# Linear attention and two MLPs on one core: weight conversion in halves, the order of the first loads, the due times of the combining sums, and the last product's steps

## The chip, the cores and the metric

One core of one Trainium2 chip. The metric is device time in microseconds (us) of one execution, the median of several.

## What is computed

```python
# q, k, v: (8, 8, 576, 64) float32
q_s = exp(q - max(q, -1));  q_s /= sum(q_s, -1) + 1e-9          # over the head's 64 columns
k_s = exp(k - max(k, 2));   k_s /= sum(k_s, 2) + 1e-9           # over the 576 positions
x   = q_s @ (k_s^T @ v)                                         # linear attention, -> 4608 x 512
h   = x @ w_in;  g = h * clip(h + 3, 0, 6) / 6;  y = g @ w_out  # 512 x 2048, 2048 x 512
xn  = y / sqrt(mean(y*y, -1) + 1e-6) * rms_g
out = (silu(xn @ w_gate) * (xn @ w_val)) @ w_out2               # 512 x 1536 (two), 1536 x 512
```

The five weight matrices arrive as 64-bit floating-point numbers (two 32-bit words each); q, k and v are float32.

## The kernel before

Every float32 product is made of three matmuls on values split in a high and a low part ("hi" and "lo", `xh`/`xl`, `phu`/`plu`, `gh`/`gl`, `uh`/`ul`): high by high, low by high, high by low. ScalarE (ACT) makes the high part by a cast (line 215), VectorE (DVE) or GpSimd (POOL) the low part by a subtraction (line 221).

The 4608 tokens are nine blocks of 512. One batch of the attention (`kv_tasks`, line 1069) loads five tiles of k (`k_0` to `k_4`), folds them to a maximum on DVE (`km`, lines 355 to 358), transposes that on TensorE (PE; `kmt`, line 368), subtracts the maximum (lines 389, 391), takes the exponential on ACT (line 395) and multiplies with v on PE (`kvp`, line 411, 80 matmuls). `q_tasks` (line 1101) does the same for q by rows (`qm` line 503, exponential line 509, `qn` line 519, transposition `qp` line 531), and `xps` (line 551) is the attention's result of a block.

A weight tile of 128 x 512 is converted to float32 on chip in `weight` (line 1036): load of the raw pairs (`raw_*`, line 235), two ACT operations (`conv_a`, lines 258 and 259), four DVE operations each on the result of the one before (`conv_d`, lines 266 to 269: clamp, shift and mask, a two-input operation that puts the words together, mask), a multiplication (`conv_p`, line 274, POOL) and an addition (`conv_s`, line 278, DVE or POOL). There are 68 such tiles: 16 of w_in, 28 of w_out and w_out2 (both appear as `wm_out`, `w_out`), 24 of w_gate and w_val (`wm_gv`, `w_gv`).

Blocks 0 to 2 go through the first MLP directly: steps `m1` (tile `h`, line 603) and `m2` (tile `y`, line 662). Blocks 3 to 8 take a two-by-two scheme that needs seven products instead of eight for w_in (`prod1`, tiles `phx`, `phy`, `phz`, line 833). The second MLP does the same with w_gate and w_val (`prod`, tiles `pux`, `puy`, `puz`, line 851) for pairs of blocks S = 0 to 3 and the last block alone as S = 4, in 12 groups of seven products each, 60 in all. The seven products of a group share three of the four rotating PSUM banks x, y, z; between two products that reuse a bank, ACT copies (`c_copy`, line 866, here called p1) and DVE adds (`c_add`, lines 868 to 873: `c12`, `c21`, `c22`) what the bank holds, and the next product waits for that. The last product is the step `m4` (tile `o`, line 962, 12 matmuls of 128x512 each); 12 of them belong to each block, and one can run once its u is there. `swu` (line 759) are sums of w_gate and w_val tiles that the scheme multiplies with.

Order of the work: the PE's order is written out as the list `seq` (lines 986 to 1017). `merge` (line 980) puts other steps between the seven products of a group. All other work is tasks of a list scheduler, `Plan` (line 40), which replays the program by costs in us and gives each engine, as it comes free, the ready task with the earliest due time, in units of PE steps, if there is room for its buffers. What it writes down is fixed in the program: each engine then works through its list in that order, and waits in place for what it needs. An entry "FLEX" may go to POOL or to DVE. Loads are all on SyncE's (SP) queue.

## Time and profile before

| | |
|---|---|
| three runs | 1773.12, 1773.75, 1774.95 us (median 1773.75) |
| profiled execution | 1766.21 us |
| its span (first to last instruction) | 1764.3 us |
| mean granted TensorE clock | 0.992 |
| busy, share of the span | PE 96%, DVE 73%, ACT 49%, POOL 20% |
| busiest queue | SP's 16 engines 61%, 199 GB/s over the span |

The profiled execution took 1766.21 us, 1.91 us more than its span and 7.54 us less than the median of the runs. In a row of the timeline the columns are start, time from there to the end of the last instruction of the row, engine, line, operation, output and inputs, number of instructions, and in square brackets the idle time of the engine before it and what ended that. Times in windows are from the span's start. A granted clock of 1.00 is the upper of TensorE's two levels (2.4 GHz), one of 0.50 the lower (1.2 GHz).

### The profile page before, as it was taken

How to read it: one execution, taken by the hardware profiler on the slowest of the kernel's cores; microseconds unless marked ns; L12 is line 12 of the kernel's file. 1: busy time of each engine (PE TensorE's matmuls, PEld its weight loads, DVE VectorE, ACT ScalarE, POOL GpSimd, SP SyncE). 2: the span in 40 equal slices, each digit the busy share in tenths (PEclk: the TensorE clock that was granted, in tenths of full speed). 3: DMA queues.
4: the chain of work that ended last, by engine and by line, in shares of the span. 5: the costliest groups of instructions: out<-in, count | busy, mean ns of one | idle time of the engine just before them, and what ended most of it. 6: DMA issues, size and time to landing. Idle time of an engine off the chain costs nothing. (4 is left out here: it accounts for less than half of the span.)

```text
span 1764.3 us, 26397 instructions
## 1 busy us (share of the span) xinstructions
PE 1697.6 (96%) x9166; PEld 1438.2 (82%) x9166; DVE 1294.8 (73%) x2202; ACT 866.3 (49%) x2018; POOL 348.7 (20%) x326
## 2 busy tenths in 40 slices
PE   4799999999999999999999999999999999999999
PEld 3577787788888898998987777888888888888997
DVE  8999777787878787878689999445754475546564
ACT  7864546555564747545355545333432344243342
POOL 2243320011211111222123343111211121111000
PEclk9799999999999999999999999999999999999999
DMA  9646376797878788576695454535453545354752
GB/s 257 188 140 209 138 255 234 269 287 244 243 224 272 207 264 261 191 245 232 199 327 163 169 197 153 189 104 191 142 188 105 182 158 182 111 173 155 264 186 83
DMA packets 189093, 351.98 MB, mean 200 GB/s; under 512 B 26016, under 2 KB 90016, under 8 KB 188960
## 3 DMA queue, kind: packets, MB, share of 16 engines
q1 hardware_dynamic: 188960, 350.30, 61.0%
q8 instruction: 73, 1.20, 0.3%
q14 instruction: 60, 0.49, 0.1%
HBM read 285.74 MB, written 64.49 MB: 199 GB/s over the span
## 5 line engine op out<-in xcount | busy, mean ns | idle before, releaser
L962 PE MATMUL o<-wv,uh 128*128 128x512 f32 x864 | 266.5, 390 | 0.0
L962 PEld LDWEIGHTS o<-wv,uh 128*128 128x128 f32 x864 | 161.0, 188 | 32.5
L221 POOL TENSOR_TENSOR plu<-pg,phu 128x512 fp32r<-128x512 f32 (+1 forms) x63 | 85.4, 1356 | 442.5 <-ACT phu L215 403.1
L962 PE MATMUL o<-wv,ul 128*128 128x512 f32 x432 | 168.0, 389 | 0.0
L662 PE MATMUL y<-gl,hout 128*128 128x512 f32 x360 | 141.9, 394 | 4.8 <-POOL gl L221 3.9
L662 PE MATMUL y<-gh,hout 128*128 128x512 f32 x360 | 144.8, 402 | 0.8 <-DVE ysb L677 0.4
L851 PE MATMUL puy<-xhu,phu 128*128 128x512 f32 (+1 forms) x360 | 133.8, 372 | 10.8 <-DVE c12u L873 8.3
L662 PE MATMUL y<-gh,wo 128*128 128x512 f32 x432 | 143.1, 392 | 1.0 <-DMA wo<-rdout 1.0
L215 ACT ACTIVATE phu<-pg 128x512 fp32r<-128x512 f32 x240 | 130.7, 569 | 23.4 <-DMA pg<-pd 23.4
L662 PE MATMUL y<-gh,lout 128*128 128x512 f32 x360 | 141.3, 393 | 0.0
L851 PE MATMUL puy<-xlu,phu 128*128 128x512 f32 (+1 forms) x360 | 132.5, 368 | 0.0
L851 PE MATMUL puy<-xhu,plu 128*128 128x512 f32 (+1 forms) x360 | 132.5, 368 | 0.0
L866 ACT COPY c21u<-pux 128x512 f32<-128x512 f32 (+1 forms) x60 | 32.5, 541 | 194.7 <-PE pux L851 194.0
L833 PE MATMUL phy<-xhh,wh 128*128 128x256 f32 x576 | 116.9, 286 | 1.2 <-DVE c12h L873 1.1
L221 DVE TENSOR_TENSOR ul<-u,uh 128x512 fp32r<-128x512 f32 x100 | 68.6, 688 | 67.0 <-ACT uh L215 45.8
L221 DVE TENSOR_TENSOR plu<-pg,phu 128x512 fp32r<-128x512 f32 (+1 forms) x177 | 115.5, 661 | 0.9 <-ACT phu L215 0.8
L873 DVE TENSOR_TENSOR c22u<-c22u,puy 128x512 f32<-128x512 f32 (+1 forms) x60 | 37.9, 631 | 95.4 <-PE puy L851 94.9
L221 POOL TENSOR_TENSOR gl<-g,gh 128x512 fp32r<-128x512 f32 x36 | 53.2, 1483 | 272.2 <-ACT gh L215 212.7
L873 DVE TENSOR_TENSOR c21u<-c21u,puy 128x512 f32<-128x512 f32 (+1 forms) x60 | 37.9, 631 | 82.5 <-PE puy L851 82.5
L833 PEld LDWEIGHTS phy<-xhh,wh 128*128 128x128 f32 x576 | 94.6, 191 | 3.9 <-DVE c12h L873 2.0
L662 PEld LDWEIGHTS y<-gh,wo 128*128 128x128 f32 x432 | 81.3, 188 | 17.5 <-DMA wo<-rdout 1.2
L962 PEld LDWEIGHTS o<-wv,ul 128*128 128x128 f32 x432 | 81.1, 188 | 17.0
(251 smaller groups left out, 4694.1 us busy)
## 6 DMA issues: line engine op xcount, KB each, us to landing
wh<-rdh SPq DMA_DIRECT2D x126, 512.0 KB, 4.9
wv<-rdout SPq DMA_DIRECT2D x96, 512.0 KB, 4.9
pg<-pd SPq DMA_DIRECT2D x180, 256.0 KB, 3.4
wo<-rdout SPq DMA_DIRECT2D x54, 512.0 KB, 4.4
raw_out<-in_moe_w_out_dram SPq DMA_DIRECT2D x28, 512.0 KB, 5.0
rdh<-hw SPq DMA_DIRECT2D x21, 512.0 KB, 4.3
v<-in_v_dram SPq DMA_DIRECT2D x72, 128.0 KB, 5.4
xn_d<-ysb SPq DMA_DIRECT2D x36, 256.0 KB, 2.6
```

Of the source, the lines that this page charges most:

```text
L215: nc.scalar.activation(hi, src, AF.Copy)
L221: on(engine).tensor_tensor(lo, src, hi.bitcast(F32), ALU.subtract)
L662: nc.tensor.matmul(acc[j][c], w[a][:, c * P:(c + 1) * P], g[b], start=(i == 0 and n == 0), stop=(i == NF - 1 and n == 2),)
L833: nc.tensor.matmul(ps[:, z, :], w[a][:, o:o + P], x[b][:, c * HALF:(c + 1) * HALF], start=(first and z == 0 and c == 0 and m == 0), stop=( ...
L851: nc.tensor.matmul(ps, w[a][:, c * P:(c + 1) * P], x[b][c], start=(first and c == 0 and m == 0), stop=(c == 1 and m == 2), skip_group_chec ...
L866: nc.scalar.copy(cs[l, j, i, "c21"], bank(l, j, i, "x"))
L873: nc.vector.tensor_tensor(cs[l, j, i, n], t, bank(l, j, i, b), ALU.add)
L962: nc.tensor.matmul(acc["o", j][c], u[a][:, c * P:(c + 1) * P], w[b], start=(i == 0 and n == 0), stop=(i == NF2 - 1 and n == 2),)
```

## The change

1. `conv_d` works on a tile in two halves of 128x256: each of the four operations is done on the first half and then on the second, eight instructions in place of four. Its cost for the planner goes from 1.55 to 1.9 us.
2. The 24 conversions of w_gate and w_val get due times between the same start and the first product of the second MLP; before, the window ended 16 steps ahead of that product's last sixth.
3. At the start the loads of k of the first batch get the earliest due time (-9), those of q follow (-8, -8, -7.2, -7.2; before -9 and -7.2); the first weight loads, v's loads and the planner's costs and lags of loads and of `km` change with them.
4. In the seven-product groups the copy p1 and the sums that a bank waits for get due times 3 to 5 steps earlier, in both MLPs.
5. The `m4` steps are queued one by one. While S = 0 at most one is put into a group, after that at most two, up to the last group but one; before, two at a time (where the first had been ready) and none in the last three groups. `merge` has a place for a single one, after the third product. PE does the same matmuls in all.

```diff
+    HS = [slice(z * NB // 2, (z + 1) * NB // 2) for z in range(2)]
...
-        nc.vector.tensor_scalar(m, m, F64_MIN, F64_MAX, ALU.max, ALU.min)
-        nc.vector.tensor_scalar(mi, mi, 3, 0x3FFFFFFF, ALU.logical_shift_left, ALU.bitwise_and)
-        nc.vector.scalar_tensor_tensor(wi, t[:, :, 1], -(1 << 30), mi, ALU.bitwise_and, ALU.bitwise_or)
-        nc.vector.tensor_scalar(mi, wi, -(1 << 23), None, ALU.bitwise_and)
+        for h in HS:
+            nc.vector.tensor_scalar(m[:, h], m[:, h], F64_MIN, F64_MAX, ALU.max, ALU.min)
+        for h in HS:
+            nc.vector.tensor_scalar(mi[:, h], mi[:, h], 3, 0x3FFFFFFF, ALU.logical_shift_left, ALU.bitwise_and)
+        for h in HS:
+            nc.vector.scalar_tensor_tensor(
+                wi[:, h], t[:, h, 1], -(1 << 30), mi[:, h], ALU.bitwise_and, ALU.bitwise_or
+            )
+        for h in HS:
+            nc.vector.tensor_scalar(mi[:, h], wi[:, h], -(1 << 23), None, ALU.bitwise_and)
...
-        at = {2: (2, 5), 4: (2, 4, 5, 6), 6: (1, 2, 3, 4, 5, 6)}.get(len(ms), range(len(ms)))
+        at = {1: (2,), 2: (2, 5), 4: (2, 4, 5, 6), 6: (1, 2, 3, 4, 5, 6)}.get(len(ms), range(len(ms)))
...
-    wait = [(S, t, i) for S, js in enumerate(SUPER) for t in range(len(js)) for i in range(NP2)]
+    wait = [(m4, S, t, ch) for S, js in enumerate(SUPER) for t in range(len(js)) for i in range(NP2) for ch in (i, i + NP2)]
...
-                elif done.get((wait[0][0], wait[0][2]), group) < group and group < 2 * NP2 * len(SUPER) - REST:
-                    n = wait.pop(0)
-                    late = [(m4, *n), (m4, *n[:2], n[2] + NP2)]
+                elif group < 2 * NP2 * len(SUPER) - 1:
+                    while len(late) < 1 + (S > 0) and done.get((wait[0][1], wait[0][3] % NP2), group) < group:
+                        late.append(wait.pop(0))
...
-        plan.add((n, "load"), Q, 2 * DMA_US, load_w, kind, i, needs=start, due=-7 if first else d - 6, take={"w": 1}, lag=DMA_LAG)
+        plan.add((n, "load"), Q, 2 * DMA_US, load_w, kind, i, needs=start, due=-7.7 if first else d - 6, take={"w": 1}, lag=DMA_LAG)
...
-        plan.add((n, "d"), V, 1.55, conv_d, *n, needs=[(n, "a")], due=d, take=U, give={"w": 1})
+        plan.add((n, "d"), V, 1.9, conv_d, *n, needs=[(n, "a")], due=d, take=U, give={"w": 1})
...
-            plan.add((n, "k", u), Q, DMA_US, load_k, b, u, needs=start, due=e - 24 * f, take=U, spare=2 if u else 9, lag=DMA_LAG)
+            plan.add((n, "k", u), Q, 0.85, load_k, b, u, needs=start, due=e - 24 * f if e else -9, take=U, spare=2 if u else 9, lag=DMA_LAG - (not e))
...
-            plan.add((n, "load"), Q, DMA_US, load_q, j, u, needs=start, due=e - (18 - u) * f if e else -7.2 if u else -9, take=U, spare=3, lag=DMA_LAG + 2)
+            plan.add((n, "load"), Q, 0.95, load_q, j, u, needs=start, due=e - (18 - u) * f if e else -8 if u < 2 else -7.2, take=U, spare=3, lag=DMA_LAG + (2 if e else -1))
...
-        plan.add((n, "p1"), A, 0.48 if two else 0.27, c_copy, "u", S, (i, z), needs=[st[1]], due=h[1] + 1, take=U)
+        plan.add((n, "p1"), A, 0.48 if two else 0.27, c_copy, "u", S, (i, z), needs=[st[1]], due=h[1] - 2, take=U)
         for name, src, b, needs, due, more in (
-            ("u2", "c21", "y", [st[6], (n, "p1")], h[6] + 2, dict(take=U)),
-            ("v", "c21", "z", [st[5], (n, "p1")], h[5] + 2, dict(take=U)),
-            ("c22", "c22", "y", [st[7], (n, "v")], h[7] + 2, {}),
+            ("u2", "c21", "y", [st[6], (n, "p1")], h[6] - 2, dict(take=U)),
+            ("v", "c21", "z", [st[5], (n, "p1")], h[5] - 2, dict(take=U)),
+            ("c22", "c22", "y", [st[7], (n, "v")], h[7] - 3, {}),
...
-        first, last = pos[m2, 2, 0], pos[prod, 0, NP2 - 1, 0, 1] - 16
+        first, last = pos[m2, 2, 0], pos[prod, 0, 0, 0, 1]
```

The same p1, u2, v and c22 lines change in `c_tasks`. Since every due time and cost feeds one planner, instructions move on all engines. Three places follow; the number behind a tile's name is the program's own.

**The start, VectorE and ScalarE.** VectorE's first rows before, and then with the change (`km` folds a tile of k, `qm` is the row maximum of a tile of q):

```order
1 L503 TENSOR_REDUCE qm_0_141<-q_0_115 128x8
2 L503 TENSOR_REDUCE qm_1_143<-q_1_121 128x8
3 L355 TENSOR_TENSOR km_83<-k_0_129 128x256
4 L356 TENSOR_TENSOR km_156<-km_83 128x128
5 L503 TENSOR_REDUCE qm_2_159<-q_2_125 128x8
6 L503 TENSOR_REDUCE qm_3_161<-q_3_127 128x8
7 L355 TENSOR_TENSOR km_83<-k_1_131 128x256
8 L356 TENSOR_TENSOR km_156<-km_83 128x128
9 L355 TENSOR_TENSOR km_83<-k_2_133 128x256
10 L356 TENSOR_TENSOR km_156<-km_83 128x128
```

```order
1 L361 TENSOR_TENSOR km_83<-k_0_115 128x256
2 L362 TENSOR_TENSOR km_131<-km_83 128x128
3 L361 TENSOR_TENSOR km_83<-k_1_121 128x256
4 L362 TENSOR_TENSOR km_131<-km_83 128x128
5 L361 TENSOR_TENSOR km_83<-k_2_125 128x256
6 L362 TENSOR_TENSOR km_131<-km_83 128x128
7 L361 TENSOR_TENSOR km_83<-k_3_127 128x256
8 L362 TENSOR_TENSOR km_131<-km_83 128x128
9 L364 TENSOR_TENSOR km_131<-km_131,k_4_129 64x512
10 L509 TENSOR_REDUCE qm_0_154<-q_0_134 128x8
11 L378 TENSOR_REDUCE kx_156<-kmt_149 128x4
12 L509 TENSOR_REDUCE qm_1_170<-q_1_138 128x8
```

The five tiles of k come first now, and q's maxima behind them. On ScalarE the rows around the second batch's exponentials, before and then with the change (line 509 or 515 is the exponential of a q tile, 395 or 401 of a k tile, 258 and 259 the two conversion operations):

```order
39 L215 ACTIVATE hin_0_531<-w_in_0_438 128x512
40 L610 ACTIVATE g_0_539<-h_0_482,half 128x512
41 L610 ACTIVATE g_1_555<-h_1_516,half 128x512
42 L258 ACTIVATE wm_in_0_561<-raw_in_0_495 128x512
43 L259 ACTIVATE wl_in_0_562<-raw_in_0_495 128x512
44 L509 ACTIVATE q_1_396,qs_1_574<-q_1_396,qm_1_553 128x64 x8
45 L215 ACTIVATE hin_1_600<-w_in_1_507 128x512
46 L509 ACTIVATE q_2_428,qs_2_611<-q_2_428,qm_2_559 128x64 x8
47 L382 COPY kmb_652<-kmb_606 128x512
48 L544 COPY qT_0_656<-qp_0_622 128x512
49 L509 ACTIVATE q_3_435,qs_3_666<-q_3_435,qm_3_572 128x64 x8
50 L395 ACTIVATE k_4_327<-k_4_327 64x512
```

```order
38 L214 ACTIVATE hin_0_519<-w_in_0_431 128x512
39 L616 ACTIVATE g_0_521<-h_0_470,half 128x512
40 L616 ACTIVATE g_1_542<-h_1_506,half 128x512
41 L515 ACTIVATE q_0_426,qs_0_549<-q_0_426,qm_0_540 128x64 x8
42 L214 ACTIVATE hin_1_574<-w_in_1_483 128x512
43 L515 ACTIVATE q_1_444,qs_1_576<-q_1_444,qm_1_544 128x64 x8
44 L388 COPY kmb_625<-kmb_587 128x512
45 L515 ACTIVATE q_2_492,qs_2_629<-q_2_492,qm_2_568 128x64 x8
46 L401 ACTIVATE k_4_365<-k_4_365 64x512
47 L401 ACTIVATE k_0_327<-k_0_327 128x512
48 L401 ACTIVATE k_1_341<-k_1_341 128x512
49 L401 ACTIVATE k_2_354<-k_2_354 128x512
```

The conversion of `raw_in_0_495`, in front of three of q's exponentials and all of k's before, now stands behind k's (not shown, the next pair after `k_3` is `raw_in_0_559`), and one q exponential less stands ahead of `k_4`.

**The first product with w_out, GpSimd.** Rows before, and then with the change (`gl_0` is the low part that the first matmul of `y` waits for, line 274 or 280 the conversion's multiplication):

```order
68 L274 TENSOR_TENSOR wl_out_1684<-wl_out_1684,wm_out_1683 128x512
69 L274 TENSOR_TENSOR wl_out_1725<-wl_out_1725,wm_out_1724 128x512
70 L274 TENSOR_TENSOR wl_out_1851<-wl_out_1851,wm_out_1850 128x512
71 L221 TENSOR_TENSOR gl_0_1894<-g_0_539,gh_0_1865 128x512
72 L274 TENSOR_TENSOR wl_out_1971<-wl_out_1971,wm_out_1970 128x512
73 L278 TENSOR_TENSOR w_out_1976<-w_out_1976,wl_out_1971 128x512
```

```order
68 L280 TENSOR_TENSOR wl_out_1660<-wl_out_1660,wm_out_1659 128x512
69 L280 TENSOR_TENSOR wl_out_1754<-wl_out_1754,wm_out_1753 128x512
70 L280 TENSOR_TENSOR wl_out_1800<-wl_out_1800,wm_out_1799 128x512
71 L220 TENSOR_TENSOR gl_0_1969<-g_0_521,gh_0_1937 128x512
72 L280 TENSOR_TENSOR wl_out_1923<-wl_out_1923,wm_out_1922 128x512
73 L280 TENSOR_TENSOR wl_out_1995<-wl_out_1995,wm_out_1994 128x512
```

`gl_0` has moved ahead of one multiplication.

**The second MLP, S = 0, VectorE.** Between the last sum of one group (`c21u_10`) and the first sum of the next (`c12u_11`), before and then with the change:

```order
1383 L873 TENSOR_TENSOR c21u_10_10678<-c21u_10_10678,puy_10_10670 128x512
1384 L266 TENSOR_SCALAR wm_gv_0_0_10725<-wm_gv_0_0_10725 128x512
1385 L267 TENSOR_SCALAR wm_gv_0_0_10725<-wm_gv_0_0_10725 128x512
1386 L268 SCALAR_TENSOR_TENSOR w_gv_0_0_10824<-raw_gv_0_0_10661,wm_gv_0_0_10725 128x512
1387 L269 TENSOR_SCALAR wm_gv_0_0_10725<-w_gv_0_0_10824 128x512
1388 L266 TENSOR_SCALAR wm_out_10820<-wm_out_10820 128x512
1389 L267 TENSOR_SCALAR wm_out_10820<-wm_out_10820 128x512
1390 L268 SCALAR_TENSOR_TENSOR w_out_10840<-raw_out_10771,wm_out_10820 128x512
1391 L269 TENSOR_SCALAR wm_out_10820<-w_out_10840 128x512
1392 L873 TENSOR_TENSOR c12u_11_10856<-c21u_11_10838,puy_11_10829 128x512
```

```order
1395 L879 TENSOR_TENSOR c21u_10_10960<-c21u_10_10960,puy_10_10951 128x512
1396 L220 TENSOR_TENSOR plu_11_4_11077<-pg_11_4_10998,phu_11_4_11063 128x256
1397 L284 TENSOR_TENSOR w_out_11005<-w_out_11005,wl_out_10979 128x512
1398 L220 TENSOR_TENSOR plu_20_1_11093<-pg_20_1_11033,phu_20_1_11079 128x512
1399 L879 TENSOR_TENSOR c12u_11_11106<-c21u_11_11095,puy_11_11082 128x512
```

Two conversions (eight instructions) stood there before; now there are two residuals and the end of a conversion.

## Rows read from the trace of the kernel before

**Rows 1.** Windows by stage: us, busy us per engine, clock, DMA.

```profile
0.00:104.00 104.00, 67.20 (x453) 50.85 (x454) 90.45 (x178) 81.75 (x282) 29.64 (x59) 0.90 0.77 208
104.00:400.00 296.00, 284.28 (x1382) 233.50 (x1383) 244.00 (x396) 161.39 (x380) 66.08 (x64) 0.99 0.67 225
400.00:930.00 530.00, 527.95 (x3510) 471.31 (x3510) 422.81 (x761) 289.46 (x721) 99.98 (x97) 1.00 0.76 243
930.00:1100.00 170.00, 160.22 (x693) 128.92 (x692) 164.42 (x249) 92.12 (x166) 68.03 (x45) 1.00 0.50 166
1100.00:1764.00 664.00, 658.01 (x3134) 553.66 (x3132) 373.15 (x622) 241.55 (x472) 85.00 (x63) 1.00 0.48 161
```

**Rows 2.** Waits of PE: us in total, times, longest us.

```profile
PE puy L851 <- DVE c12u L873: 8.3, 7, 2.6
...
PE y L662 <- POOL gl L221: 3.9, 1, 3.9
...
PE qp L531 <- DVE qn L519: 2.7, 1, 2.7
```

**Rows 3.** Timeline of PE, the start.

```profile
13.10 1.09 PE L368 MATMUL kmt<-ident,km 128*128 128x128 f32 x4 [13.10 <-DVE qs L514]
...
20.50 5.97 PE L411 MATMUL kvp<-v,k 128*64 128x65 f32 x80 [4.42 <-DMA raw_in<-in_moe_w_in_dram]
...
48.10 1.12 PE L368 MATMUL kmt<-ident,km 128*128 128x128 f32 x4 [7.78 <-DVE km L358]
...
103.88 0.38 PE L551 MATMUL xps<-qT,kvz 128*128 128x128 f32 x1 [2.77 <-DVE xl L221]
```

**Rows 4.** Timeline of DVE, the start: first tiles of q and k.

```profile
3.45 1.39 DVE L503 TENSOR_REDUCE qm<-q 128x8 f32<-128x512 f32 x2 [3.45 <-DMA q<-in_q_dram]
8.07 0.42 DVE L355 TENSOR_TENSOR km<-k 128x256 f32<-128x256 f32 x1 [3.22 <-DMA k<-in_k_dram]
```

**Rows 5.** Timeline of ACT, before and at the second batch's exponentials.

```profile
48.20 0.68 ACT L258 ACTIVATE wm_in<-raw_in 128x512 f32<-128x512 f32 x1 [6.59 <-DMA raw_in<-in_moe_w_in_dram]
...
58.76 2.71 ACT L395 ACTIVATE k<-k 64x512 f32<-64x512 f32 x5
```

**Rows 6.** Timeline of DVE, the start: a weight conversion.

```profile
21.18 0.41 DVE L266 TENSOR_SCALAR wm_in<-wm_in 128x512 f32<-128x512 f32 x1
...
22.09 0.69 DVE L268 SCALAR_TENSOR_TENSOR w_in<-raw_in,wm_in 128x512 int32<-128x512 int32 x1
22.81 0.43 DVE L269 TENSOR_SCALAR wm_in<-w_in 128x512 int32<-128x512 int32 x1
```

**Rows 7.** Timeline of DVE near the end: instructions of 128x256, and the last residuals.

```profile
1728.25 0.42 DVE L929 TENSOR_TENSOR u<-u,c12u 128x256 f32<-128x256 f32 x1
1728.59 0.42 DVE L929 TENSOR_TENSOR u<-u,c21u 128x256 f32<-128x256 f32 x1
...
1740.75 1.89 DVE L221 TENSOR_TENSOR ul<-u,uh 128x512 fp32r<-128x512 f32 x3
```

**Rows 8.** Timeline of POOL before the first product with w_out.

```profile
184.13 1.27 POOL L274 TENSOR_TENSOR wl_out<-wl_out,wm_out 128x512 f32<-128x512 f32 x1 [5.98 <-DVE wm_out L269]
186.26 1.26 POOL L221 TENSOR_TENSOR gl<-g,gh 128x512 fp32r<-128x512 f32 x1 [0.87 <-DVE w_out L278]
```

**Rows 9.** Windows behind two waits of PE, columns as in Rows 1.

```profile
188.00:191.00 3.00, 3.00 (x9) 2.33 (x8) 0.69 (x1) 0.77 (x2) 0.00 (x0) 0.50 0.23 85
270.00:273.00 3.00, 2.57 (x7) 1.78 (x6) 2.96 (x5) 3.00 (x12) 0.00 (x0) 0.50 0.85 297
```

**Rows 10.** Timeline of DVE before PE's longest wait in S = 0.

```profile
968.04 0.41 DVE L266 TENSOR_SCALAR wm_gv<-wm_gv 128x512 f32<-128x512 f32 x1
...
973.90 0.68 DVE L873 TENSOR_TENSOR c12u<-c21u,puy 128x512 f32<-128x512 f32 x1
```

**Rows 11.** Instructions on wm_gv alone, 925 to 1100 us: busy by engine.

```profile
925.00:1100.00 175.00, 9.92 (x16) 1.97 (x3) 5.64 (x4) 1.00 0.51 171
```

**Rows 12.** Chain of work that ended last, its last piece of PE.

```profile
1738.27 21.80 PE o L962 x96
```

More of the change, by code (lines that the diff above doesn't have):

```diff
@@ L31 @@
 TRAIL = 6
-REST = 3
 XP = 4
@@ L1014 @@
                 group += 1
-    for n in wait:
-        seq += [(m4, *n), (m4, *n[:2], n[2] + NP2)]
+    seq += wait
     pos = {step: h for h, step in enumerate(seq)}
@@ L1084, in kv_tasks @@
         for u in (C, *range(C)):
-            plan.add((n, "v", u), Q, DMA_US, load_v, b, u, needs=start, due=e - 16 * f + u % C * f if e else -6,
+            plan.add((n, "v", u), Q, 1.1, load_v, b, u, needs=start, due=e - 16 * f + u % C * f if e else -7.5,
                      take={"vt" if u == C else "v": 1}, lag=DMA_LAG + 2)
```

10 lines of the change are left out of this document (5 added, 5 removed).

## Prediction

> **What bounds the kernel now.** I read the windows by stage first, to see where TensorE is not busy [rows 1]. It is idle 36.8 us of the first 104 (104.00 less 67.20), 11.7 us from 104 to 400, 2.1 us from 400 to 930, 9.8 us from 930 to 1100 (the second MLP's first pair, S = 0) and 6.0 us after that: 66.4 us in all. The rest of the span is matmuls that the change neither adds nor takes away. So the most that any new order can win is those 66 us and what the lower clock costs behind the waits; of the last 6.0 us, 4.2 lie behind the last matmul (1738.27 + 21.80 = 1760.07 to the span's end at 1764.3) [rows 12]. Then the waits of TensorE, to see what ended the idle time: in S = 0 sums on VectorE that a bank waits for (`puy` behind `c12u`, 8.3 us in 7 waits), in the first MLP one wait for GpSimd's `gl` (3.9) and one for `qn` (2.7) [rows 2]. The start's timeline has four large ones: 13.10, 4.42, 7.78 and 2.77 us [rows 3]. Last the windows behind single waits: after those at 187.58 and 269.44 the granted clock is 0.50, the lower of the two levels, for some 3 us each [rows 9], so such a wait costs more than its own length.
>
> **The start.** Before, q's four tiles are queued ahead of k's. The first q tile is there at 3.45 us, the first k tile only at 8.07 [rows 4], and the chain k, `km`, `kmt`, exponentials, `kvp` sets when TensorE begins. With k first, its first tile should be there when q's first was, at about 3.45. Five tiles come at the pace at which they move: nine tiles were queued before, k's first as the fifth, so one tile takes about (8.07 - 3.45) / 4 = 1.15 us, and the fifth k tile (half as large) would be there at about 7.6 and folded at about 8.5. `kmt` comes near 8.7 in place of 13.10: 4.4 us. What is late next: q's loads stand behind k's now, and q's maxima and exponentials lose those 4 to 5 us; ScalarE, on which both kinds of exponentials run, loses its early start. `kvp` waits for ScalarE's k exponentials behind those of q, so I pass on about half: `kvp` at 18.1 in place of 20.50. The second batch: before, ScalarE stood 6.59 us in front of one conversion whose raw words came late, with q's and k's exponentials queued behind it, which began at 58.76 [rows 5]. The order now puts that conversion behind them. Following VectorE's and ScalarE's lists by hand with these durations, the second `kmt` comes at 43.7 (before 48.10 [rows 3]) and the first block's steps end about 4 us earlier. VectorE is 90.45 us busy of the 104 [rows 1], its work up to there is nearly the same, so I take no more than **-4** for the chain. The wait of 2.77 at 103.88 loses its place, since the order now puts an `h` step ahead of that `xps`: **-2**. Bounds: nothing but q's delay passed on, +2 (one q tile's exponentials of 2.7 us stand on ScalarE less its present idle); and the first 4.4 passed on whole, all of the 2.8, and half of the second batch's 7.78 besides, -11.
>
> **104 to 400.** TensorE's wait at the first `y` is one for `gl` on GpSimd, which stood behind a conversion's multiplication that itself had waited 5.98 us for VectorE, and then started at 186.26 [rows 8]. In the new order `gl` stands ahead of that multiplication. The wait is 3.9 us [rows 2], and the lower clock behind it costs half of the 3.00 us of matmuls in that window, 1.5 [rows 9]: 5.4 together, of which I take **-5** (`gl` may still wait for a buffer). The wait for `qn` is 2.7 and half of 2.57, 1.3, behind it: 4.0. There q's maxima and quotients stand some us earlier against TensorE's steps in the new order; I take **-3**. Bounds of both: 0 and -9.4.
>
> **400 to 930.** VectorE takes some of the conversions of w_gate and w_val that stood in S = 0. It is busy 422.81 of 530 us now [rows 1]; four conversions of 2.5 us and their sums are 15 us, spread over this and the stage before. There is room of over 100 us, and TensorE waits for 2.1 only. **0.**
>
> **Second MLP, S = 0.** Here VectorE is 164.42 of 170 us busy [rows 1] and its order decides. The longest wait ends with `c12u` at 973.90, before which two whole conversions stand, from 968.04 on [rows 10]. In the new order no whole conversion is between these two sums. After 925 us, 16 instructions on `wm_gv` (four conversions) take 9.92 us of VectorE and 5.64 of GpSimd [rows 11]. All leave this stage; with their additions (4 x 0.7) and four `swu` sums about 15 us of VectorE's 164 go, 9%. The last-product steps are spread, one to a group in place of two in every second, so that the need for `ul` is more even, and the sums get earlier due times. Twelve conversions of w_out2 stay. Of the 9.8 us of idle time I take **-6**; bounds -2.6 (the one longest wait) and -9.8.
>
> **After 1100.** Of 6.0 us, 1.8 are waits; the earlier sums may take some: **-0.5**, bounds 0 and -1.8. At the end, 96 matmuls in 21.80 us stand behind the last group now [rows 12]; 48 of them move ahead into the last groups, where they take the same time. What is lost is cover: VectorE's last `ul` ends at 1742.64 (1740.75 + 1.89) [rows 7], 4.4 us behind the last product. Two steps that need nothing of the last group are 2 x 12 x 21.80 / 96 = 5.45 us, so the cover just holds: **0**, to +1.6 if one residual is late.
>
> **Halves.** A conversion's four instructions run from 21.18 to 23.24, each on the result of the one before; from the first to the third start are 0.91 us for two of 0.43 [rows 6]. Instructions of 128x256 that don't depend on each other start 0.34 us apart, and three whole ones of a like kind in 1.89 us, 0.60 apart [rows 7], so width costs 0.26 per 256 and an instruction 0.08. The eight of a conversion alternate between halves, so each has one other between itself and its source. Then the two-input pair costs 0.68, and the six others, which run at 0.42 where a two-input one takes 0.69, about 0.2 each: 1.9 us in place of 2.0. That is nothing to speak of where VectorE is not late: **0**. The other bound is that each half waits for its source as a whole one does: 0.12 us more in each of eight, 0.96 less what is saved, +0.85 us a conversion.
> The Trainium skill, "VectorE: DVE Perf Modes", section on the TRN2 errata, speaks against this part: it has a fixed latency per instruction between instructions and wants tiles of 512 elements or more. The 128x256 rows do not show that latency between independent instructions; by the rule the sum would be that of the second rival below.
>
> **New stalls.** Every list is new. The small waits that TensorE has from 104 to 930 make 13.8 us, of which I removed 8 by name; another order has its own. Bounds 0 and +12; I take a quarter, nearest to what 400 to 930 shows: **+3.5**.
>
> **Sum:** -4 - 2 - 5 - 3 - 6 - 0.5 + 3.5 = **-17 us**. The profiled execution took 1766.21, so its like would take 1749; it lies 7.5 below the median of the runs, 1773.75, which goes to **1757** (1756.75).
>
> **Rivals.**
> 1. *The start gains nothing.* Q's exponentials are later by what k's gain, and VectorE's 90 us of work in 104 decide. For it: VectorE's load there, and that `kvp` at 20.50 waits behind ScalarE, not for `kmt`. Against: the 6.59 us of idle ScalarE go. The six us are lost: 1763.
> 2. *Halves cost more.* Each waits for its source: +0.85 a conversion. Six conversions stand on the start's VectorE chain, +5, and twelve in S = 0 add 10 us to VectorE, of which half reaches TensorE since 15 went: +5. Sum -7: 1767. Against it: the alternation, and the rows of 128x256. Beside it stands the Trainium skill's rule on small tiles, cited above.
> 3. *Sums ahead of residuals, slower.* With due times 3 to 5 steps earlier a sum can be put on VectorE before the product it reads is done; VectorE waits in place, and the residual `plu` of the next products behind it is late. Place: the 48 groups after 1100 us. Price: a wait of TensorE for VectorE is 8.3 / 7 = 1.2 us in the row that is nearest [rows 2]. Fourteen such waits use up the 17 us, from 18 on it is slower by over 0.2%; in half of the groups it is 24 x 1.2 = 29: 1786. For it: VectorE's list is strictly in order. Against: VectorE is busy 373 of 664 us there [rows 1], 6 us idle to a group, so a late residual has room to catch up.
>
> **How the numbers follow.** Forecast 0.62, first rival 0.20, second 0.10, third 0.08. The terms are independent, so their reaches to either bound go together as the root of the sum of squares: 5, 1.4, 3.8, 1.3 and 3.5 make 7 down; 8, 8, 3.4, 0.5, 1.6 and 8.5 make 15 up, of which two thirds are taken, since all bounds there are cases in which a part does nothing. The forecast's own range is so -24 to -7, or 1750 to 1767. To hold 8 in 10, the range reaches a little over the second rival, 1749 to 1769. About 0.2%, 3.5 us, is what can be told from no change. Faster by more: the forecast, nearly all of the first rival and half of the second, 0.85. Within: the remainders of these and the third where few waits come, 0.08. Slower: 0.07.
>
> **What would show it.** In the profile after: `kmt` near 9 us and `kvp` near 18; no 6.6 us of idle ScalarE before 50 us; no granted clock of 0.50 near 188 and 270, and no wait of `y` for `gl` above 1 us; VectorE near 150 of 170 us in S = 0 and TensorE idle under 5 there; a conversion in about 1.9 us; 48 `o` matmuls in the last 11 us. Wrong would be: TensorE idle over 35 us before 104; new waits `puy` or `phy` behind `plu` or `wh`; conversions of 2.8 us.

## The result, and the profile after

The changed kernel took 1746.26 us (median of four runs, 1744.73 to 1748.48), the kernel before 1773.43 on the same chip (1772.17 to 1774.95): a ratio of 0.9847, with a 95% interval of 0.983 to 0.9864. That is 27 us faster; 17 were forecast, and 1746 lies under the range's lower end, 1749. In a second comparison, beside other kernels, it was 1747.47 against 1771.78, a ratio of 0.9874 [0.9857, 0.989]. The profiled execution took 1746.05 us, 20.2 less than that of before (1766.21), so some 7 of the 27 us are not in the two profiles. The experiments trace most of these to the lower clock behind TensorE's waits.

The windows by stage of the changed kernel, for [rows 1]:

```profile
0.00:104.00 104.00, 74.25 (x473) 54.33 (x473) 91.42 (x234) 87.08 (x291) 31.29 (x56) 0.90 0.78 216
104.00:400.00 296.00, 288.97 (x1459) 240.93 (x1458) 251.95 (x504) 166.37 (x391) 76.08 (x68) 0.99 0.72 237
400.00:930.00 530.00, 527.63 (x3469) 470.35 (x3468) 432.98 (x875) 289.21 (x717) 120.75 (x102) 1.00 0.76 243
930.00:1100.00 170.00, 164.71 (x715) 133.37 (x715) 148.19 (x260) 86.45 (x158) 54.90 (x37) 1.00 0.50 170
1100.00:1744.00 644.00, 639.50 (x3056) 539.19 (x3054) 363.52 (x607) 235.51 (x462) 82.75 (x61) 1.00 0.47 158
```

TensorE is idle 29.8 us before 104 (before 36.8), 7.0 from 104 to 400 (11.7), 2.4 to 930 (2.1), 5.3 from 930 to 1100 (9.8) and 4.5 after (6.0). VectorE went from 164.42 to 148.19 us in the fourth stage.

TensorE's waits (us in total, times, longest us), for [rows 2]:

```profile
PE kmt L374 <- DVE km L364: 14.7, 2, 9.4
PE kvp L417 <- ACT k L401: 7.8, 2, 4.2
PE h L609 <- DVE g L619: 4.2, 2, 3.2
PE puy L857 <- DVE c22u L879: 2.8, 4, 1.4
PE o L968 <- DVE ul L220: 2.2, 3, 1.1
...
PE puy L857 <- DVE c12u L879: 0.9, 1, 0.9
```

`puy` behind `c12u` fell from 8.3 us to 0.9. The wait of `y` for GpSimd is gone, the one for `qn` at the third q tile of block 3 too. New are 2.2 us of `o` behind `ul` and a wait of `h` for `g` of 3.2 us (before, 1.4 at most).

The start on TensorE and the first rows of VectorE, for [rows 3] and [rows 4, 6]:

```profile
9.43 1.08 PE L374 MATMUL kmt<-ident,km 128*128 128x128 f32 x4 [9.43 <-DVE km L364]
...
19.17 5.96 PE L417 MATMUL kvp<-v,k 128*64 128x65 f32 x80 [4.16 <-ACT k L401]
...
45.52 1.09 PE L374 MATMUL kmt<-ident,km 128*128 128x128 f32 x4 [5.24 <-DVE km L364]
...
71.39 4.49 PE L417 MATMUL kvp<-v,k 128*64 128x65 f32 x60 [3.61 <-ACT k L401]
```

```profile
3.50 0.43 DVE L361 TENSOR_TENSOR km<-k 128x256 f32<-128x256 f32 x1 [3.50 <-DMA k<-in_k_dram]
...
8.60 0.68 DVE L364 TENSOR_TENSOR km<-km,k 64x512 f32<-64x512 f32 x1
...
18.65 0.48 DVE L267 TENSOR_SCALAR wm_in<-wm_in 128x256 f32<-128x256 f32 x2
19.05 0.49 DVE L269 TENSOR_SCALAR wm_in<-wm_in 128x256 int32<-128x256 int32 x2
19.46 0.75 DVE L271 SCALAR_TENSOR_TENSOR w_in<-raw_in,wm_in 128x256 int32<-128x256 int32 x2
20.13 0.48 DVE L275 TENSOR_SCALAR wm_in<-w_in 128x256 int32<-128x256 int32 x2
20.53 1.27 DVE L509 TENSOR_REDUCE qm<-q 128x8 f32<-128x512 f32 x2
```

The first k tile is there at 3.50 (before 8.07), `kmt` runs at 9.43 (before 13.10), `kvp` at 19.17 (20.50), the second `kmt` at 45.52 (48.10). A conversion in halves starts its four pairs at 18.65, 19.05, 19.46 and 20.13 and the next instruction at 20.53: 1.88 us.

The first product of the second MLP (`pux`) divides the program into two parts that can be compared one by one. The group of the `pux` matmuls, by operation and tile, gives its time (line, engine, operation, count, shortest, median and longest ns, first and last start, shapes), before and changed:

```profile
L851 PE MATMUL pux<-xhu,phu x240: 277/389/398, 915.1 to 1736.3; 128*128 128x512 f32 x96, 128*128 128x256 f32 x24
```

```profile
L857 PE MATMUL pux<-xhu,phu x240: 278/389/793, 901.6 to 1726.6; 128*128 128x512 f32 x96, 128*128 128x256 f32 x24
```

| execution profiled | first `pux` | from there to the span's end |
|---|---|---|
| before, first profile (1766.21 us) | 915.1 | 849.2 |
| before, second (1775.27) | 924.1 | 849.2 |
| before, third (1770.21) | 917.4 | 850.7 |
| before, fourth (1772.20) | 919.6 | 850.8 |
| changed, first (1746.05) | 901.6 | 842.5 |
| changed, second (1746.02) | 901.7 | 842.4 |

### The profile page after: what moved, and what is told of

Its sections match the earlier page's. It is cut to its first block, busy times and chain, and to the rows that moved or that the text cites. A ratio compares the mean times of both kernels' runs of the same rounds, so it can differ in the third digit from the quotient of the medians.

```text
span 1744.1 us, 26721 instructions
## 1 busy us (share of the span) xinstructions
PE 1695.1 (97%) x9166; PEld 1438.2 (82%) x9166; DVE 1288.1 (74%) x2478; ACT 864.6 (50%) x2018; POOL 365.8 (21%) x322
## 4 chain that ended last, share of the span: by engine, by line
PE 82%; DVE 7%; issue 2%; ACT 1%; DMA 1%; POOL 0%; SPq 0%; DVEq 0%; POOLq 0%; ACTq 0%
PE y L668 19%; PE o L968 16%; PE puy L857 12%; PE pux L857 8%; PE puz L857 8%; PE phy L839 6%; PE phz L839 4%; PE phx L839 4%; PE h L609 3%; PE kvp L417 1%; PE xps L565 1%; DVE w_out L271 1%; DVE g L619 1%; DMA wg_in<-wd_in 1%; PE rs L698 0%
## 5 line engine op out<-in xcount | busy, mean ns | idle before, releaser
L220 POOL TENSOR_TENSOR plu<-pg,phu 128x512 fp32r<-128x512 f32 (+1 forms) x58 | 75.1, 1295 | 424.6 <-ACT phu L214 360.6
L220 DVE TENSOR_TENSOR ul<-u,uh 128x512 fp32r<-128x512 f32 x103 | 72.7, 705 | 69.1 <-ACT uh L214 47.0
L515 ACT ACTIVATE q<-q,qm 128x64 f32<-128x64 f32 x256 | 85.2, 337 | 13.9 <-DVE qm L509 11.3
```

Of the source, the lines that this page charges most:

```text
L220: on(engine).tensor_tensor(lo, src, hi.bitcast(F32), ALU.subtract)
L515: nc.scalar.activation(t, t, AF.Exp, bias=m[:, g, :], accum_out=sm[:, g, :])
```

## The experiments

In each case "changed" is the changed kernel, and the edit is made to it unless said otherwise. Times are medians; for single executions the profile's.

| kernel | us | before, beside it | ratio, 95% interval |
|---|---|---|---|
| changed, again | 1747.47 | 1771.78 | 0.9874 [0.9857, 0.989] |
| whole tiles in the conversion (part 1) | 1748.88 | 1771.93 | 0.9864 [0.9839, 0.9889] |
| old window of conversions (part 2) | 1750.79 | 1771.93 | 0.9877 [0.9852, 0.9902] |
| old loads, due times and costs (part 3) | 1759.34 | 1771.93 | 0.9926 [0.990, 0.9951] |
| old due times of loads | 1751.43 | 1773.24 | 0.9871 [0.9849, 0.9893] |
| old costs of loads and `km` | 1755.81 | 1773.63 | 0.9903 [0.9874, 0.9932] |
| old due times of sums (part 4) | 1749.86 | 1771.78 | 0.9884 [0.9869, 0.9898] |
| old last-product steps (part 5) | 1744.82 | 1771.78 | 0.9853 [0.9838, 0.9868] |
| before with part 3 alone | 1756.67 | 1773.24 | 0.9899 [0.9879, 0.992] |
| before, waits filled | 1768.66 | 1773.24 | 0.9975 [0.9963, 0.9987] |
| changed, waits filled | 1743.71 | 1771.78 | 0.9846 [0.9827, 0.9866] |
| changed, part 5 undone, waits filled | 1740.09 | 1773.24 | 0.9805 [0.9784, 0.9826] |

The interval of the changed kernel (0.983 to 0.9864, and again 0.9857 to 0.989) overlaps those of the kernels with whole tiles, the old window, the old due times of loads, the old sums and the old last-product steps. By the intervals these five can't be told from it; what is said below of their size rests on medians and on one profile each. With all of part 3 undone the interval lies clear of both, with the old costs alone of the first.

### The kernel before, three more profiles

No edit.

> The kernel before, a second profile. The two profiled executions differ by 20.2 us (1766.21 and 1746.05), the medians by 27.2. Theory: the first profiled execution of before was a short one, and a usual one holds some 7 us more in one or two places that can be found by setting the two traces side by side; a new profile then shows about 1773. Rival: profiling itself shortens this kernel; then the new profile is near 1766 again, with the same stalls.

> The kernel before, a third profile. In the second, the first product of the second MLP came at 924.1 us in place of 915.1 and the end as long after it (849.2 us in both): 9.0 us more, of which I count 4 to 5 as the lower clock (behind the waits at 104.91, 191.16, 274.04 and 401.50), 1.7 as a longer wait for wo and the rest as small waits. Theory: a usual execution has its excess before that product, some 4 to 9 us of it, in these places. Rival: it lies elsewhere each time.

> The kernel before, a fourth profile, with the same question. Theory: the excess over the first profile lies before the first product of the second MLP, in the same waits and the lower clock behind them. Rival: it lies elsewhere each time.

They took 1775.27, 1770.21 and 1772.20 us. So the first profile, 1766.21, was a short execution: of the kernel before's 43 timed ones none was shorter. In all three, TensorE waits in the same places, but the granted clock behind the waits is not the same. Windows of 3 us behind the wait that ends near 104 us (us, busy us per engine, clock, DMA), first profile and third:

```profile
102.00:105.00 3.00, 1.12 (x5) 0.86 (x6) 2.97 (x7) 1.74 (x4) 1.59 (x1) 1.00 0.01 3
105.00:108.00 3.00, 3.00 (x15) 2.47 (x14) 2.16 (x5) 2.83 (x6) 0.00 (x0) 1.00 0.92 283
108.00:111.00 3.00, 3.00 (x16) 2.44 (x15) 1.89 (x4) 2.60 (x5) 0.00 (x0) 1.00 0.72 273
```

```profile
102.00:105.00 3.00, 1.39 (x5) 1.09 (x5) 3.00 (x6) 2.01 (x4) 1.59 (x1) 0.64 0.02 5
105.00:108.00 3.00, 3.00 (x8) 2.16 (x7) 1.64 (x4) 2.48 (x5) 0.00 (x0) 0.50 0.99 323
108.00:111.00 3.00, 3.00 (x11) 2.37 (x10) 0.69 (x1) 0.61 (x2) 0.00 (x0) 0.72 0.31 117
```

and the waits on both sides of this stretch, `h` in the first (its `xps` stood at 103.88), then both in the third:

```profile
136.70 0.50 PE L603 MATMUL h<-xh,hin 128*128 128x512 f32 x1 [0.84 <-DVE g L613]
```

```profile
103.61 2.07 PE L551 MATMUL xps<-qT,kvz 128*128 128x128 f32 x4 [2.81 <-DVE xl L221]
...
139.31 0.50 PE L603 MATMUL h<-xh,hin 128*128 128x512 f32 x1 [0.84 <-DVE g L613]
```

The wait is 2.8 us in both ([rows 3] and here), the clock behind it 1.00 in the first and 0.50 in the third. From there to the `h` step's wait it is 32.82 us in the first (136.70 - 103.88) and 35.70 in the third: 2.9 more; in the second and fourth, which have 0.50 and 0.60 behind the wait, it is 34.32 and 34.37, 1.5 more. The same holds at the wait of 2.6 us in S = 0: the first profile (and the second) kept 1.00, the third and fourth fell to 0.66 and 0.57 in a window of 3 us, and took 1.5 us longer from the first `pux` to the end. Ahead of the `xps`, from the `h` near 82 us on, the three take 1.0, 0.6 and 1.1 us more than the first, with no new wait; in the second and fourth the clock stays at 0.50 some 3 us longer there. The rest of the second profile's 9.0 us are 1.0 behind `y`'s wait, 1.7 of a longer wait for a load of w_out near 400 us, the lower clock behind that (1.9, with one small wait), and small waits. The theory holds in part: of the excess over the first profile, 9.0 of 9.0, 2.3 of 3.8 and 4.5 of 6.1 us lie before the first `pux`. The 2.3 is less than the 4 to 9 expected, and the places and sizes change from one execution to the next.

### The changed kernel again

No edit.

> The changed kernel again, beside the others of this call and before. Theory: the usual execution of before is slowed by stretches at the lower clock behind waits that the change takes away, so the changed kernel runs at 0.992 to 0.994 in all its executions, within 3 us of 1746, and before at 0.984 to 0.991 between 1766 and 1780: a ratio near 0.985. Rival: the 27 us of the first comparison are a chance of four runs each, and the ratio comes nearer to the profiles' own, 0.9886.

Its executions, 1746.02 to 1749.65, are at 0.991 to 0.993 in mean clock, those of before beside them, 1768.32 to 1774.36, at 0.985 to 0.990. The clocks are as the theory has them, within 0.001; one execution lies 3.7 us above 1746 where 3 were allowed. The ratio, 0.9874 [0.9857, 0.989], is not: its interval holds the rival's 0.9886 and not the theory's 0.985. Over both comparisons the gain is 24 to 27 us by the medians and 22 to 27 by the ratios. The second comparison alone does not exclude the profiles' 20; that the usual gain is larger rests on the three profiles above and the filling below.

### Filling TensorE's waits, before and changed

```diff
+    def fill(n, dst=None):
...
+        for _ in range(n):
+            nc.tensor.matmul(dst, kvbd[0][0][:, 0, :], w[:, :dst.shape[-1]], start=True, stop=True)
...
     def k_tr(b):
         kmp[b] = ptile(f"kmt{b}", (P, C, P))
+        if b == 1:
+            fill(26)
```

and so at the other places that the expectation names; `kvbd[0][0]` holds zeros then. VectorE, ScalarE, GpSimd and the queues keep their lists.

> The kernel before, in its own order, with matmuls on zeros in six of TensorE's waits: in front of the first kvp (12 of 512 columns), the second batch's kmt (26), the third kvp (11), the xps that waits at 103.88 (10), the first y (14) and the third qp of block 3 (10). No other engine's list changes. Theory (what the profile of before did not show is the lower clock behind these waits, longer or shorter from one execution to the next): mean clock up from 0.984 to 0.991 to 0.994 or more, the time 8 to 13 us below before, 1759 to 1764, and the executions closer together than before's 6 us or more. Rival (the executions differ by the arrival of loads, or by VectorE and GpSimd getting in each other's way): clock up, time within 3 us of before, the spread the same.

Measured 1768.66 us, 4.6 less than before beside it (2.3 to 6.6 by the ratio's interval), mean clock 0.993 to 0.995 (before 0.985 to 0.990). This speaks against the rival, which allowed 3 us, and the theory was too large: 8 to 13 were expected. The 11 executions lie within 5.5 us (1766.75 to 1772.2), 16 of before within 12.6 (1768.73 to 1781.3), but within 7.6 without the longest one; that filling narrows the spread is not shown. The filling at the second `kmt` left 2.0 us of its wait, and the clock still fell behind it. In the profile the `xps` near 104 us comes no sooner (VectorE's `xl` ends its wait), but the stretch behind it has the first profile's length again, 32.83 us:

```profile
103.63 1.14 PE L570 MATMUL xps<-qT,kvz 128*128 128x128 f32 x4 [0.47 <-DVE xl L221]
...
136.46 0.50 PE L622 MATMUL h<-xh,hin 128*128 128x512 f32 x1 [0.83 <-DVE g L632]
```

Its first `pux` comes at 915.8 (915.1 in the first profile, 917.4 to 924.1 in the others). So filling the waits gives back what the usual executions lose ahead of it, 4.6 us. This is a net figure and no exact share of the 7: two of the filled waits had the lower clock in the first profile too [rows 9], and waits came elsewhere (2.2 us in `y` at 217.68). The rest, with the second profile's longer load, stays open.

> The changed kernel with matmuls on zeros in three of TensorE's waits at the start: 24 of 264 columns before the first kvp, 18 of 512 before the second batch's kmt, 24 of 264 before the third kvp. They write what the real matmuls then overwrite, and should end before the awaited data come. Theory (the lower clock follows an idle TensorE, and costs time by itself): the two stretches at 0.50 behind 42 and 69 us shorten or go, and the time falls by 3 to 8 us against the changed kernel of this call. Rival (VectorE and ScalarE set the start's pace, the lower clock there is hidden): the clock is up and the time within 2 us. Second rival (the added matmuls delay the real ones): slower by 2 us or more.

Here 1743.71, against 1747.47 for the changed kernel beside it: 3.8 less, mean clock 0.994 to 0.997. Windows behind the second `kmt`, the changed kernel and then this one:

```profile
45.00:48.00 3.00, 1.69 (x7) 1.32 (x8) 2.89 (x7) 3.00 (x18) 0.00 (x0) 0.50 0.83 198
48.00:51.00 3.00, 3.00 (x10) 2.43 (x9) 2.86 (x9) 3.00 (x18) 0.00 (x0) 0.50 1.01 341
...
72.00:75.00 3.00, 3.00 (x46) 2.53 (x45) 3.00 (x11) 3.00 (x9) 0.00 (x0) 0.50 0.02 5
```

```profile
45.00:48.00 3.00, 1.87 (x12) 1.46 (x11) 2.96 (x8) 3.00 (x17) 0.00 (x0) 1.00 0.93 271
48.00:51.00 3.00, 3.00 (x16) 2.46 (x16) 2.86 (x9) 3.00 (x18) 0.00 (x0) 1.00 1.10 287
...
72.00:75.00 3.00, 2.98 (x22) 2.08 (x18) 2.90 (x13) 3.00 (x18) 0.81 (x2) 1.00 0.72 246
```

The clock column goes from 0.50 to 1.00. In its profile, the shortest of its four executions (1740.02 to 1746.01), the first `pux` comes at 895.7, 5.9 us sooner. So the lower clock at the start does cost the changed kernel time by itself, even where VectorE is busy nearly all the time (2.86 to 3.00 of 3 us in these windows).

### Part 3 undone, alone, and by halves

```diff
-            plan.add((n, "k", u), Q, 0.85, load_k, b, u, needs=start, due=e - 24 * f if e else -9, take=U, spare=2 if u else 9, lag=DMA_LAG - (not e))
+            plan.add((n, "k", u), Q, DMA_US, load_k, b, u, needs=start, due=e - 24 * f, take=U, spare=2 if u else 9, lag=DMA_LAG)
...
```

and the other lines of part 3 in the same way.

> The changed kernel with the loads' old due times and costs at the start (part 3 undone), all else as changed. Theory: the start gave 7.0 of the 20.2 us between the profiles (TensorE idle before 104 us: 36.8 and 29.8); without it 1746 + 5 to 8 = 1751 to 1754, kmt at 13 us. Rival: the start's gain came from the other parts (the new plan as a whole, by way of VectorE), and the loads' order is worth nothing: 1746 to 1748, though kmt is at 13.

1759.34 us, some 12 over the changed kernel: more than the theory's 5 to 8. `kmt` ran at 13 us. Idle time before 104 is 32.6 us, only 2.8 more; from 104 to 400 it is 13.3, 6.3 more. A wait of 5.8 us that the changed kernel hasn't:

```profile
266.33 0.76 PE L668 MATMUL y<-gh,hout 128*128 128x512 f32 x1 [5.77 <-ACT gh L214]
```

`gh` stood on ScalarE behind exponentials of q and casts for other products. Then each half of the part was undone alone, the due times and lags of the first loads (as in the lines of the change, costs left as changed):

```diff
-            plan.add((n, "k", u), Q, 0.85, load_k, b, u, needs=start, due=e - 24 * f if e else -9, take=U, spare=2 if u else 9, lag=DMA_LAG - (not e))
+            plan.add((n, "k", u), Q, 0.85, load_k, b, u, needs=start, due=e - 24 * f, take=U, spare=2 if u else 9, lag=DMA_LAG)
...
```

> The changed kernel with only the due times and lags of the first loads as before, and the planner's costs of loads and of km as changed. Undoing both cost 12 us, of which 2.8 us are idle time of TensorE before 104 us and 6.3 from 104 to 400 (two waits of y for gh behind q's exponentials). Theory: the due times make the part before 104 us and the clock behind it, the costs the waits after it: 1750 to 1753, without those y waits. Rival: any shift at the start leads to such waits, 1757 or above. Second rival: it is all costs, 1746 to 1748.

and the planner's costs of loads and `km` (due times left as changed):

```diff
-            plan.add((n, "k", u), Q, 0.85, load_k, b, u, needs=start, due=e - 24 * f if e else -9, take=U, spare=2 if u else 9, lag=DMA_LAG - (not e))
+            plan.add((n, "k", u), Q, DMA_US, load_k, b, u, needs=start, due=e - 24 * f if e else -9, take=U, spare=2 if u else 9, lag=DMA_LAG - (not e))
...
-            plan.add((n, "km", u), V, 0.72 if u < C else 0.61, k_max, b, u, needs=[(n, "k", u)] + ([(n, "km", u - 1)] if u else []),
+            plan.add((n, "km", u), V, 0.56 if u < C else 0.61, k_max, b, u, needs=[(n, "k", u)] + ([(n, "km", u - 1)] if u else []),
...
```

> The changed kernel with the planner's old costs of loads and km, and the new due times of the first loads: the other half of part 3. Undoing all of part 3 cost 12.6 us, undoing the due times alone 4.7. Theory (the costs are worth the other 8 us, through the plan of 104 to 400): 1753 to 1757, with a wait of y behind q's exponentials. Rival (the two only work together or the order is a matter of luck): 1746 to 1750.

By the medians the due times alone cost 4 to 5 us (1751.43), the costs alone 8 to 10 (1755.81); by the ratios 0 to 4 and 5 to 10. In the profiles the first `pux` comes at 906.5 and 914.0 (changed 901.6), and behind it both take 842.1. So the times are as both theories have them, but the mechanism of the due times is not. `kmt` is at 12.97 again, yet TensorE's idle time before 104 us is 30.7, only 0.9 more than in the changed kernel; from 104 to 400 it is 9.3, 2.3 more, with waits of `y` of which the theory had none (3.1 us for `gl`, 3.6 for `ysb`).

With the old costs there are two waits of `y`, 4.9 us at the first one and 3.2 at 377 us. The first stands where the kernel before had its wait, but GpSimd is through with the conversion's multiplication at 176.53 and then stands 5.18 us; what ended this, by the profile, is the store of an earlier `g` to memory (timeline of GpSimd and TensorE):

```profile
175.24 1.29 POOL L280 TENSOR_TENSOR wl_out<-wl_out,wm_out 128x512 f32<-128x512 f32 x1 [1.98 <-PE h L609]
181.72 1.26 POOL L220 TENSOR_TENSOR gl<-g,gh 128x512 fp32r<-128x512 f32 x1 [5.18 <-DMA g_d<-g]
```

```profile
183.03 0.80 PE L668 MATMUL y<-gl,hout 128*128 128x512 f32 x1 [4.89 <-POOL gl L220]
```

In the changed kernel `gl` starts 6.6 us sooner:

```profile
175.09 2.11 POOL L220 TENSOR_TENSOR gl<-g,gh 128x512 fp32r<-128x512 f32 x1 [8.40 <-ACT gh L214]
177.17 1.28 POOL L280 TENSOR_TENSOR wl_out<-wl_out,wm_out 128x512 f32<-128x512 f32 x1
```

With the old due times the first `y` doesn't wait either. So that it waits for nothing comes from the costs of loads and `km` in the planner, that are in force throughout the program, and not from the loads' order at the start. And the other way round, the kernel before with all lines of part 3 and nothing else:

> The kernel before with part 3 alone (the first loads' due times and all the planner's costs of loads and km). Theory: kmt near 9.4 us, and of the 12 us that undoing it cost at least the 3 to 6 us of the start: 8 to 13 us below before, 1759 to 1764. Rival (part 3 pays only with the others, whose plan keeps VectorE free): within 4 us of before.

1756.67, 16.6 us below before: more than the theory. In its profile the first `pux` comes at 904.0 (changed: 901.6) and the rest takes 849.7, as before. TensorE is idle 29.3 us before 104. So part 3 by itself is enough for nearly all that was won ahead of the second MLP.

### Parts 1, 2, 4 and 5 undone

Whole tiles (the order of all engines is the same):

```diff
-    HS = [slice(z * NB // 2, (z + 1) * NB // 2) for z in range(2)]
+    HS = [slice(0, NB)]
```

> The changed kernel with whole tiles in the conversion and everything else as changed, the order of all five engines the same. Theory (halves are nothing to speak of, 0.1 us of VectorE a conversion): within 2 us of the changed kernel, 1744 to 1749, and a conversion takes 2.0 us in place of 1.9. Rival (halves matter at the start and in S = 0, where VectorE is late): 3 us or more slower, 1749 or above. Second rival (halves cost): 3 us or more faster, below 1743.

1748.88: inside what the theory allows, and its interval holds the changed kernel's ratio; halves gain some 2 us or nothing, and no cost of them is seen. In the profile a whole conversion's instructions start 0.44 to 0.72 us apart:

```profile
20.07 0.41 DVE L267 TENSOR_SCALAR wm_in<-wm_in 128x512 f32<-128x512 f32 x1
20.51 0.43 DVE L269 TENSOR_SCALAR wm_in<-wm_in 128x512 int32<-128x512 int32 x1
20.98 0.69 DVE L271 SCALAR_TENSOR_TENSOR w_in<-raw_in,wm_in 128x512 int32<-128x512 int32 x1
21.70 0.43 DVE L275 TENSOR_SCALAR wm_in<-w_in 128x512 int32<-128x512 int32 x1
```

Old window for the conversions of w_gate and w_val:

```diff
-        first, last = pos[m2, 2, 0], pos[prod, 0, 0, 0, 1]
+        first, last = pos[m2, 2, 0], pos[prod, 0, NP2 - 1, 0, 1] - 16
```

> The changed kernel with the old window of due times for the conversions of w_gate and w_val (part 2 undone), all else as changed. Theory: the four conversions come back into S = 0 and with them most of the 4.5 us that TensorE's idle time lost there (9.8 and 5.3): 1749 to 1752. Rival: the earlier sums and the spread steps made that gain: 1746 to 1748.

1750.79, as the theory has it in size; but from the first `pux` on it takes 844.1 us, only 1.6 more than the changed kernel, so not most of the gain there.

Old due times of the sums:

```diff
-        plan.add((n, "p1"), A, 0.48 if two else 0.27, c_copy, "u", S, (i, z), needs=[st[1]], due=h[1] - 2, take=U)
+        plan.add((n, "p1"), A, 0.48 if two else 0.27, c_copy, "u", S, (i, z), needs=[st[1]], due=h[1] + 1, take=U)
```

and the other three as before, in both MLPs.

> The changed kernel with the old due times of the copy p1 and the sums (part 4 undone), all else as changed. Theory: they made the part of the gain in S = 0 that the conversions' window did not, and the small waits at 1274 and 1454: 1748 to 1750. Rival: without them the waits of puy for c12u return in full, 8 us: 1752 or above. Second rival: worth nothing, 1745 to 1747.

1749.86, 2.4 over the changed kernel beside it (their four executions overlap); from the first `pux` on 845.3, or 2.8 more. `puy` waits for `c12u` 6.0 us in place of 0.9, most in one place:

```profile
1076.00 0.60 PE L857 MATMUL puy<-xhu,phu 128*128 128x512 f32 x1 [2.30 <-DVE c12u L879]
```

Old last-product steps:

```diff
-    wait = [(m4, S, t, ch) for S, js in enumerate(SUPER) for t in range(len(js)) for i in range(NP2) for ch in (i, i + NP2)]
+    wait = [(S, t, i) for S, js in enumerate(SUPER) for t in range(len(js)) for i in range(NP2)]
...
-                elif group < 2 * NP2 * len(SUPER) - 1:
-                    while len(late) < 1 + (S > 0) and done.get((wait[0][1], wait[0][3] % NP2), group) < group:
-                        late.append(wait.pop(0))
+                elif done.get((wait[0][0], wait[0][2]), group) < group and group < 2 * NP2 * len(SUPER) - 3:
+                    n = wait.pop(0)
+                    late = [(m4, *n), (m4, *n[:2], n[2] + NP2)]
...
```

> The changed kernel with the last product's steps as before, in pairs and eight behind the last group (part 5 undone), all else as changed. Theory: worth 0 to 2 us, in S = 0 alone: 1746 to 1748, with the new waits of o for ul (2.2 us in 3) gone. Rival: the even spread is what lets VectorE keep up in S = 0: 1749 or above. Second rival: the spread costs what those waits show, 1744.

1744.82, 2.65 less than the changed kernel beside it, and the four runs (1742.85 to 1745.81) lie under all of its (1746.02 to 1749.65): by these, part 5 costs some 2 us. From the first `pux` on it takes 840.1 in place of 842.5. Of this, TensorE's waits from 900 to 1100 are 4.7 us in place of 6.0. The waits of `o` for `ul`, which the theory had gone, are still there with pairs (2.4 us in two, against 2.2 in three). What differs is `puy`: with pairs it waits once in this stretch (1.66, behind `c12u`), with single steps more often:

```profile
966.66 0.50 PE L857 MATMUL puy<-xhu,phu 128*128 128x512 f32 x1 [0.91 <-DVE c12u L879]
...
971.08 0.50 PE L968 MATMUL o<-wv,ul 128*128 128x512 f32 x1 [0.93 <-DVE ul L220]
...
979.15 0.50 PE L857 MATMUL puy<-xhu,phu 128*128 128x512 f32 x1 [1.39 <-DVE c22u L879]
```

The other 1 us was not found.

### A version faster than both

Part 5 undone as above, and four waits filled, the fourth in the `h` steps:

```diff
     def m1(j, i):
+        nth.append(0)
+        if len(nth) == 25:
+            fill(12)
...
```

> The changed kernel without part 5 (the last product's steps as before) and with matmuls on zeros in four waits: first kvp (11 of 512 columns), second batch's kmt (18), third kvp (12), the h step that waits 3.2 us near 146 us (12). Theory (both gains add, 2.7 for part 5 and 3.8 for the filling, some more for the h step): 1738 to 1742, ratio to before 0.981 to 0.983. Rival (they overlap, as both runs were on a good day): 1743 or above.

1740.09 us, a ratio of 0.9805 [0.9784, 0.9826] to before, five runs from 1737.04 to 1742.18; the clock is 0.997 to 1.0. So the gains add, within the scatter; the changed kernel was not run beside it.

## Why the prediction was wrong, step by step

**The step that failed** is the last line of the sum: "it lies 7.5 below the median of the runs, 1773.75, which goes to 1757". It takes the distance of one profiled execution from the median for a property of the measurement. It was one of that execution: before's other three profiles lie within 4 us of the median, and the changed kernel's two within 1.5 of theirs. Of the 10.5 us between 1756.75 and 1746.26 this step makes 7.3 (7.5 for before, 0.2 for the changed kernel), and the sum 3.2. What the first profile lacked is in good part the lower clock behind its larger waits, which came in some executions and not in others: behind the `xps` near 104 us (1.5, 2.9 and 1.5 us in three profiles, 0 in the first) and the `puy` in S = 0 (0, 1.5, 1.5), and 0.6 to 1.1 us ahead of that `xps` and up to 1 us behind the first `y`, more than in the first. That is some 5 us in each of the three, with the 1.9 near 400 us in the second. I priced it at two waits alone, those where the trace showed 0.50 [rows 9], 1.5 and 1.3 us. The change removes these waits, and with them what they cost in the usual execution; filling such waits gave 4.6 us. That `xps`' wait of 2.77 was priced at -2, with nothing for the clock, is the clearest place.

**The sum itself** was nearly right between the two first profiles: -17 forecast, -20.2 measured; before the first `pux` -10.5 (the start -6, two waits -8, new stalls +3.5) against -13.5, after it -6.5 against -6.7.

- *The start, -6.* TensorE's idle time before 104 us fell by 7.0, and part 3 alone makes that (29.3 us idle). `kmt` came at 9.43 where I had 8.7, `kvp` at 19.17 (18.1), the second `kmt` at 45.52 (43.7): the chain by hand was 0.7 to 1.8 us too quick, in part as the third k tile came late (VectorE waited for it 1.47 us). The size was right, but that the earlier first `kmt` makes it is not shown: with the old due times `kmt` is at 12.97 again and the idle time 30.7, with the old costs 9.05 and 30.6, with neither 32.6, still 4.2 less than before. How the lines of part 3 work together here stays open. That part 3 alone is worth 12 to 17 us I did not see: I read it as an order of four loads, and its larger half is the planner's costs, 8 to 10 us, by way of waits as far as 377 us.
- *104 to 400, -8, and new stalls, +3.5.* Both waits (3.9 and 2.7) went, as the order had shown, and others came (3.2 in `h`, 1.9 in `y` are the longest): idle from 104 to 930 fell from 13.8 to 9.4, by 4.4, so 2.2 of the 6.6 came back. The charge was near. That the first `y` waits for nothing, which I took from the order, hangs on the costs.
- *S = 0 and after, -6.5.* Right in size, -6.7. The shares were not: the window gives 1.6, the due times of the sums 2.8, and the single steps, from which I hoped for an even need of `ul`, take 2.4 back. That makes 2.0; whole tiles (842.2 us from the first `pux` on) and the old loads (842.5) change nothing there, so the other 4.7 us come with no one part and were not traced. Idle time in S = 0 is 5.3 us where under 5 was to show it.
- *The end, 0.* Behind the last group's product 48 matmuls run from 1728.59 on without a pause (chain that ended last):

```profile
1728.59 10.92 PE o L968 x48
```

- *Halves, 0.* 1.88 us a conversion, 1.9 forecast. The rule of the Trainium skill, "VectorE: DVE Perf Modes", section on the TRN2 errata, that small tiles pay a fixed latency, did not make the halves slower here: with another instruction between each half and its source, eight halves took 1.88 us and four whole ones 1.98 (20.07 to the next instruction at 22.05). Halves without that were not tried.

**The rivals.** That the start gains nothing falls with the runs on part 3. That halves cost more falls with the whole tiles, which were not faster. That sums ahead of residuals make it slower falls with the old due times, which were no faster (2.4 us slower in the median), and no wait of `puy` or `phy` for `plu` or `wh` is in the profile after.

## What to carry to other kernels

One profile shows the waits well and their price badly, where the clock may or may not fall behind them: take two or three profiles of the kernel before, mark what differs, and price the longer waits with the lower clock behind them. Where a planner's cost of an operation is changed, look for its effect over the whole program and not where the diff puts it. A wait that can't be removed may still be filled: matmuls on zeros into a bank that is overwritten gave 3.8 and 4.6 us here.
